# Splitting the first bank's products into upper and lower row halves in eleven pieces of a sequence transform

## The chip, the cores and the metric

The kernel runs on one core of one Trainium2 chip. The core has a matrix engine (TensorE, PE in the profile, with its weight loads listed apart as PEld), and the engines VectorE (DVE), ScalarE (ACT), GpSimd (POOL) and SyncE (SP), which issues most DMA transfers. The metric is the device time of one execution in microseconds; a smaller time is better. Times of several executions are given as a median.

## The reference

The output mixes two branches by a gate for each of 2048 tokens of 640 features. Cut to what matters:

```python
g = sigmoid((x * gate_w).sum(-1, keepdims=True))
# A: a Fourier mixing by matrices, real part of DFT_seq(DFT_hidden(x))
a = x @ dft_hid_re.T ; b = x @ dft_hid_im.T
A = dft_seq_re @ a - dft_seq_im @ b
# B: an expert layer: for 32 heads the best two of 16 + 16 keys, four candidates,
# the best two of them, softmax, and gelu(x . u[expert]) * v[expert]
out = g * A + (1 - g) * B
```

The kernel works out A in the other order, first along the sequence and then along the features. The change lies in the first of these two products, `dft_seq_re @ x`.

## The kernel before

All products are made in a split form: each operand f is held as a high part h and a rest l, both in a 32-bit matmul format, and a product is the sum of three matmuls, wh with h, wh with l and wl with h. The helper `mm3` (L141) issues the three into one PSUM bank; its lines L143, L144 and L145 are most of TensorE's work.

The sequence transform is cut into 128 pieces `n = (w, c, s)` (L170): w is the real or imaginary matrix, c one of four chunks of 512 output positions, s one of 16 blocks of 128 input tokens. In `seq_piece` a piece takes the 128 tokens as rows of the array: the weights are the tokens' features `X[s]` (128 columns for each of five feature blocks d), the moving operand is a 128 x 512 block of the matrix, h and l. Bank d (0 to 4) collects feature block d over the 16 pieces of a chunk. So a piece issues 5 x 3 = 15 matmuls, and behind the last piece of a chunk ScalarE copies each bank to a staging tile `ST`.

The first four pieces (`BYPASS`) issue their products in another order (L239), part by part over all five banks, while the inputs are still coming in. From piece 4 on the order is bank by bank.

The order of the work is written out by hand: the program's order is the order on each engine. `seq_piece(n)` issues the load for piece n + 5 (SP queue), the split for piece n + 3 (ScalarE and GpSimd), and the products of piece n; `follow(n)` then issues what a table (`at`) has put behind piece n. In the first 30 pieces that is: loading and splitting the tokens (`load_x`, `split_x`), sums for the gate (`gate_sum`, VectorE), and behind pieces 6, 9, 12, 15 and so on, up to piece 27, the weight folding `w_part`: 16 matmuls from `wq` tiles that fill 32 columns of the array each (L380, listed as 32 in the trace), whose results VectorE transposes (L386). `load_wq` (L371) fetches the next `wq` tiles into buffers that these matmuls free. From piece 31 on, steps of the expert branch are put between the pieces (`score_step`), and later products of one-hot tiles that fill 64 columns (L857).

PSUM has eight banks. Banks 0 to 4 belong to the sequence transform, 5 and 6 to `w_part`; bank 7 holds the warm-up products at the start and is taken again by the expert branch from piece 31 on. The staged results of the first chunk are multiplied by the gate on VectorE behind piece 23 (`gate_piece`, L217).

Of the kernel before, what the change touches and what calls it, by code (L numbers as in the profile page):

```python
# [17 lines left out]
P = 128  # L18
# [7 lines left out]
NT = S // P  # L26
# [15 lines left out]
AWAY = 11  # L42
BYPASS = 4
ACCUM_END = NT * (NC + 2) - 4


class Pump:
# [59 lines left out]
def gated_mix_kernel(ctx: ExitStack, tc: tile.TileContext, xT, xn, dreT, dimT, wsre, wsim, wq, kT, uT, vv, gw, out):  # L107
    nc = tc.nc
# [13 lines left out]
    def bank(n, shape=(P, TC), dt=F32):  # L122
        return psum.tile(list(shape), dt, name=f"b{n}", tag=f"b{n}")
# [9 lines left out]
    def stage():  # L133
        return ST[:, rotate("st", 5)]

    def split(f, h, l, eng):

        nc.scalar.activation(h, f, AF.Copy)  # L138
        eng.tensor_sub(l, f, h.bitcast(F32))  # L139

    def mm3(o, wh, wl, ah, al, first, last, more=False):  # L141

        nc.tensor.matmul(o, wh, ah, start=first, stop=False, skip_group_check=more)  # L143
        nc.tensor.matmul(o, wh, al, start=False, stop=False, skip_group_check=more)  # L144
        nc.tensor.matmul(o, wl, ah, start=False, stop=last, skip_group_check=more)  # L145
# [9 lines left out]
    def run_bg(us):  # L155
        bg.run(us, share)
# [14 lines left out]
    pf, psp, X, xr = {}, {}, {}, {}  # L171

    def load_piece(n):
        if n < NPC:
            w, c, s = pieces[n]
            pf[n] = big.tile([P, TC], F32, name="wf", tag="wf", bufs=5)
            nc.sync.dma_start(pf[n], (wsre, wsim)[w][c, s])  # L177
# [3 lines left out]
    def split_piece(n):  # L181
        if n < NPC:
            psp[n] = h, l = WS[:, n % 4, 0], WS[:, n % 4, 1]
            f = pf.pop(n)
            if not N0 + 4 <= n < (4 * NT if n % 2 else ACCUM_END) or 4 * NT <= n < N1 + 10:
                split(f, h, l, nc.gpsimd)
                return
            nc.scalar.activation(h, f, AF.Copy)
            nc.scalar.activation(l, h.bitcast(F32), AF.Copy, scale=-1.0)  # L189
            w, c, s = pieces[n]  # L190
            nc.gpsimd.dma_start(l, (wsre, wsim)[w][c, s], accum_op=OP.add)  # L191
# [9 lines left out]
            f()  # L201


    banks = []
    p3, last_part, ending, closing, early, share = None, False, False, False, True, 0.95
    grow, staged, P22 = {}, {}, {}

# [21 lines left out]
    def seq_piece(n):  # L229
        w, c, s = pieces[n]  # L230
        if s == 0:
            banks[:] = [bank(d) for d in range(KD)]
        load_piece(n + 5)
        split_piece(n + 3)
        h, l = psp.pop(n)
        if n < BYPASS:
            for a, (x, c) in enumerate(((0, h), (0, l), (1, h)) if n == 0 else ((0, h), (1, h), (0, l))):
                for d in range(KD):
                    nc.tensor.matmul(banks[d], X[s][:, x, d * P:(d + 1) * P], c, start=n + a == 0, stop=False)  # L239
            return  # L240
        for d in range(KD):
            ds = slice(d * P, (d + 1) * P)
            mm3(banks[d], X[s][:, 0, ds], X[s][:, 1, ds], h, l, s == 0, s == NT - 1)
            if s == NT - 1:
                staged[n // NT, d] = f = stage()
                nc.scalar.activation(f, banks[d], AF.Copy)
            run_bg(0.68)

    for q in range(2 * NC):
        n = NT * (q + 1)  # L250
# [246 lines left out]
    n = b + 2  # L497
# [20 lines left out]
    for n in range(N0):  # L518
        seq_piece(n)
        follow(n)  # L520
# [252 lines left out]
    for p in range(NP):  # L773
        n = N0 + 4 * p + min((p + 1) // 2, 3)
# [3 lines left out]
    for n in range(2 * NT + 3, 4 * NT + 3):  # L778
        s = n % NT
# [269 lines left out]
    for k, (n, m) in enumerate(((-1, 2), (0, 4), (5, 7), (7, 9), (10, 12))):  # L1049
        n, m = NT * (NC + 2) + n, NT * (NC + 2) + m  # L1050
# [181 lines left out]
    for n in range(N0, NPC):  # L1232
        ending, closing, early = n >= NPC - 7, n % NT == NT - 1, n < ACCUM_END
        seq_piece(n)
        follow(n)
        if n >= N1 and p3 is None and NT // NB - 1 in gated:
            p2_stack.close()
            p3 = ctx.enter_context(tc.tile_pool(name="p3", bufs=1, reuse_waits="tile"))
            pools.append(p3)
            HOT.append(p3.tile([P, 2, 2, 16 * E * 4], F16, name="hot0"))  # L1240
            HOT.append(p3.tile([P, 2, 2, 16 * E * 4], F16, name="hot1", tag="WP"))
            bg.add(experts(), late=True)
            bg.credit -= 3.0
        if n == NPC - 4:
            bg.drain(lambda: {2, 3} <= set(free_sets))
            HOT.pop()
            WP = p3.tile([P, 2, 2, TC], F32R, name="WP", tag="WP")
        for m in prep_split.get(n, ()):
            split_step(m)
# [54 lines left out]
```

## Time and profile before

| what | value |
|---|---|
| median of two runs | 750.96 us (750.54 and 751.38) |
| the profiled execution, first to last instruction (span) | 748.7 us |
| its own time with what lies around the span | not listed apart; the two runs are 1.8 to 2.7 us above the span |
| granted TensorE clock, mean | 0.999 |
| full-size products in L143, L144, L145 on `X` | 3 x 620 listed |
| 32-column products (L380) | 256 in 8 blocks |
| 64-column products (L857) | 512 |

The span is that of one execution which the hardware profiler recorded. In a group's row stand line, engine, operation, output from input, array rows x columns, shape and count, and then the busy time in us, the mean length of one in ns, and the idle time ahead of them. In a timeline row stand start and length in us, then engine, line, operation and count. A matmul's listed length reaches from its start to the end of its way through the array, and the next one starts well before that; the pace is the distance between starts.

### The profile page before, as it was taken

How to read it: one execution, taken by the hardware profiler on the slowest of the kernel's cores; microseconds unless marked ns; L12 is line 12 of the kernel's file. 1: busy time of each engine (PE TensorE's matmuls, PEld its weight loads, DVE VectorE, ACT ScalarE, POOL GpSimd, SP SyncE). 2: the span in 40 equal slices, each digit the busy share in tenths (PEclk: the TensorE clock that was granted, in tenths of full speed). 3: DMA queues.
4: the chain of work that ended last, by engine and by line, in shares of the span. 5: the costliest groups of instructions: out<-in, count | busy, mean ns of one | idle time of the engine just before them, and what ended most of it. 6: DMA issues, size and time to landing. Idle time of an engine off the chain costs nothing.

```text
span 748.7 us, 11141 instructions
## 1 busy us (share of the span) xinstructions
PE 743.8 (99%) x3925; PEld 603.8 (81%) x3925; DVE 585.7 (78%) x741; ACT 365.9 (49%) x664; POOL 342.4 (46%) x286
## 2 busy tenths in 40 slices
PE   9999999999999999999999999999999999999998
PEld 7777767888888888888888888888888888888887
DVE  6964098495999899999999888979899974357651
ACT  4325234543544745555463686633545653443451
POOL 5533325440532424145235456643455793487253
PEclk9999999999999999999999999999999999999999
DMA  9999999777556786972398766488876689775301
GB/s 333 392 380 364 344 374 354 231 222 250 129 176 141 190 242 157 237 200 79 114 395 285 162 168 188 133 255 280 266 234 197 222 262 343 219 239 172 113 29 71
DMA packets 84488, 171.11 MB, mean 229 GB/s; under 512 B 16080, under 2 KB 21328, under 8 KB 84176
## 3 DMA queue, kind: packets, MB, share of 16 engines
q1 hardware_dynamic: 70960, 146.13, 57.9%
q0 software_dynamic: 5472, 9.96, 8.5%
q10 hardware_dynamic: 8000, 14.31, 5.2%
q8 instruction: 31, 0.51, 0.3%
q14 instruction: 25, 0.20, 0.1%
HBM read 136.40 MB, written 32.39 MB: 225 GB/s over the span
## 4 chain that ended last, share of the span: by engine, by line
PE 94%; DMA 5%; SPq 0%; DVE 0%; ACT 0%; issue 0%; ACTq 0%
PE b L143 30%; PE b L145 30%; PE b L144 30%; PE b L239 2%; DMA wf<-in_wsre 2%; PE b L380 2%; DMA wq<-in_wq 1%; PE b L857 1%; DMA xd<-X 1%; DMA gdr<-gc 1%; DVE wp L386 0%; SPq L177 0%; ACT WS L295 0%; ACTq L514 0%; DVE ST L1191 0%
## 5 line engine op out<-in xcount | busy, mean ns | idle before, releaser
L143 PE MATMUL b<-WS,X 128*128 128x512 f32 x620 | 243.3, 392 | 0.0
L144 PE MATMUL b<-WS,X 128*128 128x512 f32 x620 | 241.4, 389 | 0.0
L145 PE MATMUL b<-WS,X 128*128 128x512 f32 x620 | 241.3, 389 | 0.0
L139 POOL TENSOR_TENSOR WS<-wf,WS 128x512 fp32r<-128x512 f32 x89 | 131.9, 1486 | 168.3 <-ACT WS L138 151.8
L143 PEld LDWEIGHTS b<-WS,X 128*128 128x128 f32 x620 | 116.3, 188 | 28.2 <-issue 4.1
L145 PEld LDWEIGHTS b<-WS,X 128*128 128x128 f32 x620 | 116.4, 188 | 24.4
L144 PEld LDWEIGHTS b<-WS,X 128*128 128x128 f32 x620 | 116.4, 188 | 23.6
L138 ACT ACTIVATE WS<-wf 128x512 fp32r<-128x512 f32 x89 | 55.5, 626 | 69.0 <-PE b L145 40.9
L845 DVE TENSOR_TENSOR hot<-rows,wtab 128x1024 f16<-128x1024 f16 x64 | 57.8, 930 | 4.3 <-PE b L857 4.3
L139 POOL TENSOR_TENSOR xl<-xf,xh 128x640 fp32r<-128x640 f32 x16 | 27.2, 1702 | 72.0 <-ACT xh L138 72.0
L567 ACT ACTIVATE sc<-b 128x512 f32<-128x512 f32 x32 | 19.9, 621 | 80.8 <-PE b L145 77.0
L191 POOL DMA_DIRECT2D WS<-in_wsre x30 | 26.4, 881 | 61.8 <-ACT WS L189 60.5
L139 POOL TENSOR_TENSOR WS<-ra,WS 128x512 fp32r<-128x512 f32 x33 | 47.1, 1439 | 14.3 <-ACT WS L138 14.1
L815 ACT ACTIVATE b<-b,mask 128x128 f32<-128x128 f32 x128 | 43.1, 342 | 14.9 <-PE b L857 11.8
L138 ACT ACTIVATE WS<-ra 128x512 fp32r<-128x512 f32 x47 | 29.4, 631 | 42.4 <-PE b L145 29.6
L622 DVE TENSOR_TENSOR eq<-sc,mm 128x1024 f16<-128x1024 f32 x32 | 44.4, 1387 | 0.9
L629 DVE TENSOR_REDUCE tied<-eq 128x64 f32<-128x1024 f16 x32 | 39.0, 1219 | 0.9
L620 DVE TENSOR_REDUCE mm<-sc 128x64 f32<-128x1024 f32 x32 | 38.7, 1211 | 0.2
L139 POOL TENSOR_TENSOR WP<-ra,WP 128x512 fp32r<-128x512 f32 x13 | 19.2, 1490 | 31.0 <-ACT WP L138 30.9
L217 DVE SCALAR_TENSOR_TENSOR ST<-ST,grow 128x512 f32<-128x512 f32 x40 | 31.7, 855 | 1.7 <-ACT tw L138 1.7
L845 DVE TENSOR_TENSOR hot<-hot,rows 128x1024 f16<-128x1024 f16 x32 | 31.6, 986 | 0.0
L143 PE MATMUL b<-WU,xh 128*128 128x512 f32 x80 | 31.1, 389 | 0.0
(209 smaller groups left out, 1449.1 us busy)
## 6 DMA issues: line engine op xcount, KB each, us to landing
X<-xd SPq DMA_DIRECT2D x36, 640.0 KB, 6.5
wq<-in_wq SPq DMA_DIRECT2D x32, 640.0 KB, 7.1
wf<-in_wsim SPq DMA_DIRECT2D x64, 256.0 KB, 4.8
wf<-in_wsre SPq DMA_DIRECT2D x63, 256.0 KB, 6.4
ra<-pd SPq DMA_DIRECT2D x40, 256.0 KB, 3.3
pd<-ST ACTq DMA_DIRECT2D x35, 256.0 KB, 5.6
WS<-in_wsre POOLq DMA_DIRECT2D x30, 256.0 KB, 6.0
xd<-X SPq DMA_DIRECT2D x11, 640.0 KB, 9.1
```

Of the source, the lines that this page charges most:

```text
L138: nc.scalar.activation(h, f, AF.Copy)
L139: eng.tensor_sub(l, f, h.bitcast(F32))
L143: nc.tensor.matmul(o, wh, ah, start=first, stop=False, skip_group_check=more)
L144: nc.tensor.matmul(o, wh, al, start=False, stop=False, skip_group_check=more)
L145: nc.tensor.matmul(o, wl, ah, start=False, stop=last, skip_group_check=more)
L191: nc.gpsimd.dma_start(l, (wsre, wsim)[w][c, s], accum_op=OP.add)
L217: nc.vector.scalar_tensor_tensor(f, f, -1.0 if w else 1.0, g, op0=OP.mult, op1=OP.mult)
L620: nc.vector.tensor_reduce(m, sc, op=OP.max, axis=AX.X)
L622: nc.vector.tensor_tensor(eq, sc, m[:, :, None].to_broadcast([P, HH, E]), op=OP.is_equal)
L629: nc.vector.tensor_reduce(tied[:, s, ib, :], eq, op=OP.add, axis=AX.X)
L815: nc.scalar.activation(f[:, :, n], f[:, :, n], AF.Copy, scale=mask4[:, n:n + 1])
L845: nc.vector.tensor_tensor(o, a, b, op=op)
```

## The change

In pieces 4 to 14 of the first chunk (`ROW_TILED`) the three products of bank 0 are cut in two by rows. The upper 64 tokens' product goes to bank 0 as before, and the lower 64 tokens' product, which works in the lower half of the array's rows, goes to bank 7, held as `lower` from piece 4 on. Upper and lower alternate in the program. Piece 15 makes full products again. At the chunk's end, behind ScalarE's copy of bank 0 to the staging tile, VectorE adds bank 7 to it. Banks 1 to 4 and all other pieces stay.

```diff
+ROW_TILED = range(BYPASS, NT - 1)
...
-    banks = []
+    banks, lower = [], []
...
+        if n == BYPASS:
+            lower.append(bank(7))
         for d in range(KD):
             ds = slice(d * P, (d + 1) * P)
-            mm3(banks[d], X[s][:, 0, ds], X[s][:, 1, ds], h, l, s == 0, s == NT - 1)
+            if d == 0 and n in ROW_TILED:
+                top, low = slice(0, P // 2), slice(P // 2, P)
+                for i in range(3):
+                    w, a = X[s][:, i // 2, ds], (h, l, h)[i]
+                    nc.tensor.matmul(banks[0], w[top], a[top], start=False, stop=False)
+                    nc.tensor.matmul(lower[0], w[low], a[low], start=i == 0 and n == BYPASS,
+                                     stop=i == 2 and n == ROW_TILED[-1])
+            else:
+                mm3(banks[d], X[s][:, 0, ds], X[s][:, 1, ds], h, l, s == 0, s == NT - 1)
             if s == NT - 1:
                 staged[n // NT, d] = f = stage()
                 nc.scalar.activation(f, banks[d], AF.Copy)
+                if d == 0 and lower:
+                    nc.vector.tensor_add(f, f, lower.pop())
```

On TensorE, at the end of piece 6, behind which a block of 32-column products stands, and the start of piece 7. Before (b_162 to b_166 are banks 0 to 4):

```order
L145 MATMUL b_166<-WS,X 128x512
L380 MATMUL b_354<-wq,kp 32x320 x4
L380 MATMUL b_359<-wq,kp 32x320 x4
L380 MATMUL b_354<-wq,kp 32x320 x4
L380 MATMUL b_359<-wq,kp 32x320 x4
L143 MATMUL b_162<-WS,X 128x512
L144 MATMUL b_162<-WS,X 128x512
L145 MATMUL b_162<-WS,X 128x512
L143 MATMUL b_163<-WS,X 128x512
```

And now, where the lines of the pair are L250 and L251 and b_279 is bank 7:

```order
L146 MATMUL b_166<-WS,X 128x512
L393 MATMUL b_364<-wq,kp 32x320 x4
L393 MATMUL b_369<-wq,kp 32x320 x4
L393 MATMUL b_364<-wq,kp 32x320 x4
L393 MATMUL b_369<-wq,kp 32x320 x4
L250 MATMUL b_162<-WS,X 128x512
L251 MATMUL b_279<-WS,X 128x512
L250 MATMUL b_162<-WS,X 128x512
L251 MATMUL b_279<-WS,X 128x512
L250 MATMUL b_162<-WS,X 128x512
L251 MATMUL b_279<-WS,X 128x512
L144 MATMUL b_163<-WS,X 128x512
```

Three products of bank 0 have become six, and here the halves follow the 32-column block directly; in eight of the eleven pieces they stand between full products on both sides.

On VectorE, at the end of the chunk (piece 15), ahead of the transposes of the next `w_part` block. Before:

```order
L509 TENSOR_SCALAR gt<-gt 128x16
L510 STREAM_TRANSPOSE gc<-gt 128x32
L386 STREAM_TRANSPOSE wp<-b_680 128x2x5x32
L386 STREAM_TRANSPOSE wp<-b_685 128x2x5x32
L139 TENSOR_TENSOR WU<-wp,WU 128x5x128
```

And now:

```order
L522 TENSOR_SCALAR gt<-gt 128x16
L523 STREAM_TRANSPOSE gc<-gt 128x32
L259 TENSOR_TENSOR ST<-ST,b_279 128x512
L399 STREAM_TRANSPOSE wp<-b_715 128x2x5x32
L399 STREAM_TRANSPOSE wp<-b_720 128x2x5x32
L140 TENSOR_TENSOR WU<-wp,WU 128x5x128
```

One addition stands ahead of the transposes, and it waits for ScalarE's copy. The order on ScalarE, GpSimd and SyncE is the one of before.

## The prediction

> **What bounds the kernel now.** I read the page's first and fourth parts, then who waited for whom on TensorE.
>
> ```profile
> PE 743.8 (99%) x3925; PEld 603.8 (81%) x3925; DVE 585.7 (78%) x741; ACT 365.9 (49%) x664; POOL 342.4 (46%) x286
> PEclk9999999999999999999999999999999999999999
> PE 94%; DMA 5%; SPq 0%; DVE 0%; ACT 0%; issue 0%; ACTq 0%
> PE b L326 <- PEq L1296: 0.8, 1, 0.8
> PE b L380 <- DMA wq<-in_wq: 0.7, 1, 0.7
> ```
>
> TensorE (PE) is busy for 743.8 of 748.7 us at an undiminished clock, it is 94% of the chain that ended last, and it waited for others for 1.5 us in all. So a microsecond added to TensorE's stream comes out at the end almost whole, and nothing that another engine saves is seen. But a busy TensorE isn't at its peak: the real pace lies in the distances between starts. The stretch below stands at the end of piece 6, which is one of the eleven that change; in it lies one block of L380, whose products fill 32 columns of the array each, four beside each other.
>
> ```profile
> 27.59 0.39 PE L145 MATMUL b<-WS,X 128*128 128x512 f32 x1
> 27.81 0.39 PE L143 MATMUL b<-WS,X 128*128 128x512 f32 x1
> 28.04 0.39 PE L144 MATMUL b<-WS,X 128*128 128x512 f32 x1
> 28.27 0.39 PE L145 MATMUL b<-WS,X 128*128 128x512 f32 x1
> 28.59 2.36 PE L380 MATMUL b<-wq,kp 128*32 128x320 f32 x32
> 30.88 0.50 PE L143 MATMUL b<-WS,X 128*128 128x512 f32 x1
> 31.21 0.40 PE L144 MATMUL b<-WS,X 128*128 128x512 f32 x1
> 31.45 0.39 PE L145 MATMUL b<-WS,X 128*128 128x512 f32 x1
> 31.68 0.40 PE L143 MATMUL b<-WS,X 128*128 128x512 f32 x1
> 31.91 0.39 PE L144 MATMUL b<-WS,X 128*128 128x512 f32 x1
> 32.14 0.39 PE L145 MATMUL b<-WS,X 128*128 128x512 f32 x1
> 32.37 0.39 PE L143 MATMUL b<-WS,X 128*128 128x512 f32 x1
> ...
> 30.51 0.43 PE L380 MATMUL b<-wq,kp 128*32 128x320 f32 x1
> ```
>
> The first column is the start. From 27.59 to 28.27 three products take 0.68 us: one full product costs 0.227 us, not the 0.39 us of its own length. The last row, the last product of the L380 block, comes from a narrower look at the same timeline.
>
> **The change, part by part.**
>
> *Removed:* in 11 pieces the three full products of the first bank, 33 x 0.227 = 7.5 us of TensorE.
>
> *Added on TensorE:* 66 products over 64 rows with the same 512 columns. A half product streams as many columns as a full one, so the change can win nothing by streaming; the question is whether the two of a pair run beside each other. No product over half of the rows stands in this trace. The nearest row is L380, with several parts of the array working at once: from 28.59 to 30.51 stand 31 steps, so 0.062 us for each product of 320 columns. At the pace of the full products (0.227 / 512 us per column) 320 columns would take 0.142 us. More than two ran at a time, then. I take it that two row halves do the same, and a pair costs about what one product costs. At most the pair is quicker by what a full product has beyond its streaming:
>
> ```profile
> L143 PE MATMUL b<-WS,X 128*128 128x512 f32 x620 | 243.3, 392 | 0.0
> L143 PE MATMUL b<-WS,ts 128*128 128x256 f32 x8 | 2.3, 283 | 0.0
> ```
>
> 256 more columns lengthen a product by 392 - 283 = 109 ns, so 512 columns are 0.218 us of the 0.227: a gain of 0.009 x 33 = 0.3 us at most. At the other end the two halves run one after the other: 33 x 0.227 = 7.5 us more. Between these I take 0.1 us for all 33 pairs, near the gainless end, since L380 is the row that is nearest in kind.
>
> *Weight loads.* Each half product loads its own 128 columns, 66 loads for 33.
>
> ```profile
> 30.87 0.19 PEld L143 LDWEIGHTS b<-WS,X 128*128 128x128 f32 x1 [0.52 <-issue]
> 30.98 0.19 PEld L144 LDWEIGHTS b<-WS,X 128*128 128x128 f32 x1
> 31.21 0.19 PEld L145 LDWEIGHTS b<-WS,X 128*128 128x128 f32 x1
> ```
>
> After the L380 block two loads start 0.11 us apart although each is listed with 0.19, so loads follow each other every 0.11 us. Two are 0.22 us and just fit under a pair of 0.227. Normally a load starts with the product before it (31.21 stands in both lists) and is hidden there. I cost it at nothing; the cover is the pair that is running. If the loads went strictly one behind the other at 0.19, a pair would take 0.38: 33 x 0.15 = 5.0 us.
>
> The Trainium skill, TensorE: Matmul & The Clock Gate, section Part 3 (packing small matmuls), gives for tiles in different row groups a span of one product and about 4 ns more; by it the 33 pairs would cost 0.13 us. The same section says that a weight load overlaps a running product only where the row groups differ. The trace disagrees for full products, whose load at 31.21 starts together with the product before it; for halves it is a rival below.
>
> *Switches of the array's layout.* This is the term that I take to decide. The L380 block shows both directions. Into it: 28.59 - 28.27 = 0.32, 0.09 more than a product's step. Out of it: a round of four takes (30.51 - 28.59) / 7 = 0.27, but from the last product to the first full one it is 30.88 - 30.51 = 0.37, 0.10 more. Then 31.21 - 30.88 = 0.33, 0.10 more than a step, since the first load wasn't made ahead (the load at 30.87 starts with its product, after 0.52 idle). The five steps from 31.21 to 32.37 take 1.16, 0.02 to 0.03 over 5 x 0.227. Out costs 0.10 + 0.10 + 0.025 = 0.22 to 0.23 us. The other product that splits the array shows the same:
>
> ```profile
> 570.72 0.39 PE L145 MATMUL b<-WS,X 128*128 128x512 f32 x1
> 571.04 0.95 PE L857 MATMUL b<-hot 128*64 128x64 f16 x48
> 571.92 0.50 PE L143 MATMUL b<-WS,X 128*128 128x512 f32 x1
> 572.25 0.39 PE L144 MATMUL b<-WS,X 128*128 128x512 f32 x1
> ...
> 571.79 0.20 PE L857 MATMUL b<-hot 128*64 128x64 f16 x1
> ```
>
> In: 571.04 - 570.72 = 0.32 again. Out: the restart 572.25 - 571.92 is 0.33 again. The step into row halves needs loads of 128 columns like the restart: 0.09 + 0.10 + 0.02 = 0.21 to 0.22. I take 0.23 for either direction.
>
> How many: each of the 11 pieces goes into the halves at its start and out after the first bank, 22 switches. Three of these pieces (7, 10, 13) stand right behind an L380 block, whose way out was paid before too; there the halves follow the 32-column tiles directly and only one switch is new. 22 - 3 = 19, and 19 x 0.23 = 4.4 us. Bounds: nothing that the trace shows is under 0.09, which gives 1.7 us; with no price at all it is nought.
>
> The Trainium skill, TensorEngine Tiling (Array Packing), section Key Properties, says that changing the tiling mode drains TensorE, and not changing the tile within a mode. The trace agrees, with 0.32 and 0.37 us where 0.227 and 0.27 are the steps. The rule gives no price, so the sum by it is the one of the rows, 4.4 us; without a drain it would be nothing.
>
> *Added on VectorE:* one addition from PSUM at the end of the chunk, and bank 7 held from piece 4 to there. Its price is in an addition of the same kind; its place is ahead of the transposes that wait for the next L380 block:
>
> ```profile
> L1114 DVE TENSOR_TENSOR ST<-ST,b 128x512 f32<-128x512 f32 x14 | 9.4, 685 | 18.5 <-ACT ST L1110 11.0 <-PE b L145 5.0 <-ACT WS L138 2.5
> 65.07 0.21 DVE L510 STREAM_TRANSPOSE gc<-gt 128x32 f32<-128x32 f32 x1
> 68.61 1.05 DVE L386 STREAM_TRANSPOSE wp<-b 128x320 f32<-128x320 f32 x2 [3.34 <-PE b L380]
> ```
>
> 0.69 us falls into an idle stretch of 3.34 us. It waits for ScalarE's copy of the first bank; behind it stand only transposes whose products come later. The result is read in piece 23 (L217), and bank 7 isn't taken again before the scores begin. Nothing. Without that cover it would be 0.69 us of VectorE, which has a fifth of its time idle.
>
> *What is given back:* TensorE waits once for a wq transfer, 0.7 us, in the last L380 block, behind the changed pieces. If the transfer keeps its time while TensorE is 4 us later, that wait goes; but the wq loads are themselves released by the products that use them:
>
> ```profile
> 104.86 1.82 PE L380 MATMUL b<-wq,kp 128*32 128x320 f32 x24
> 107.37 0.74 PE L380 MATMUL b<-wq,kp 128*32 128x320 f32 x8 [0.69 <-DMA wq<-in_wq]
> ...
> SPq L371 <- PE b L380: 22.1, 8, 5.0
> ```
>
> The queue waited 22.1 us for that, so these loads mostly move with TensorE. Between nothing and 0.7 I take 0.2 back. The other transfers and splits get more time, not less.
>
> Sum: 4.4 + 0.1 - 0.2 = 4.3 us. The profiled execution's span goes from 748.7 to 753.0 us. The two timed runs took 750.54 and 751.38 us, so 1.8 to 2.7 us lie around the span, and the change doesn't touch them. Against the median of 750.96 the forecast is **755.3 us**. Two per cent, about what a measurement of this kernel tells from no change, is 15.0 us: the forecast is slower but within it.
>
> **The rivals.**
>
> *A, cheap switches.* If row halves only drain, with their loads made ahead, or if the layout doesn't count as another, a switch is 0.09 at most: 19 x 0.09 = 1.7 us, some of it given back, 752.5 us. Against it: both blocks of split products pay the restart. Chance 0.12.
>
> *B, loads not hidden.* In the halves a load waits until its own rows are free, while the other half runs beside it: 0.11 x 33 = 3.6 us more, 758.9 us. For it: 2 x 0.11 leaves hardly any room under 0.227. Against it: full products load under a running product in the same rows. The rule of the Trainium skill cited above on row groups would bring this about. Chance 0.10.
>
> *C, the change doesn't do what it says.* The halves run in turn: 7.5 us more, 762.8 us. Against it: L380's 0.062 us for 320 columns; for it: those are column tiles, each with all 128 rows, and no row tile was ever seen here. Chance 0.12.
>
> *D, the other side: slower by over 2%.* Every half product behaves like the first one after a switch, 0.33 from start to start with its load in the open, and the halves run in turn: 66 x 0.33 = 21.8 us for 7.5, 14.3 more, and 4.3 on top, less 11 x 0.10 that the entries already hold: 17.5 us, 768.5 us. It decides from 0.29 us per half product on (7.5 + 15.0 - 4.3 + 1.1 = 19.3 over 66). Against it: inside the L380 block the loads lie under running products. Chance 0.05.
>
> **How the numbers follow.** The forecast keeps 0.61. A, B and C lie within 2%. The range goes from 751.5 (A with the whole 0.7 given back and the 0.3 of quicker pairs: 1.7 - 1.0 = 0.7) to 763.2 (C with its 0.2 not given back, and the 0.2 by which the sum may be rounded); D and the edges of A and C stay outside. The likeliest case's own range is 753.5 to 756.5. Faster by over 2%: no case gives it, 0.01 for the unforeseen. Slower by over 2%: D, 0.05. Within: 0.94.
>
> **What would show it.** In the profile after, the two lines of a pair (its upper and its lower half) start within 0.02 us of each other and the next pair 0.23 later; pair starts 0.45 apart would be C, 0.33 with the loads idle before them B or D. The first pair of a piece should start 0.32 after the last full product, and the first full product behind the pairs should be followed by a step of 0.33. Eleven first banks should take 0.68 + 0.4 us each. The addition should stand in an idle stretch of VectorE. TensorE's wait for wq should be 0.7 or less. I would be wrong by most if a half product can't start while the other half runs, or if a switch into row halves costs another multiple of the full drain.

## The result and the profile after

| | before | after |
|---|---|---|
| median of the runs, us | 750.96 (2 runs) | 754.92 (754.72 and 755.12) |
| span of the profiled execution, us | 748.7 | 752.9 |
| ratio of times | 1 | 1.0057, 95% interval 1.0041 to 1.0073 |

The change makes the kernel slower by 0.6%, 4.0 us by the medians and 4.3 us by the two spans before rounding (748.66 and 752.94). The lines of the page of after that answer to those of before (shares of the span; engines of the chain), and who waited for whom on TensorE:

```profile
PE 748.9 (99%) x3958; PEld 603.8 (80%) x3958; DVE 585.5 (78%) x742; ACT 366.3 (49%) x664; POOL 344.7 (46%) x286
PEclk9999999999999999999999999999999999999999
PE 99%; DVE 0%; issue 0%
PE b L339 <- PEq L1309: 0.8, 1, 0.8
```

TensorE bounds the kernel as before, with 33 products more and 5.1 us more busy time, and no wait for wq is listed any more. The timeline of TensorE at the first changed piece (4), and its weight loads over the same stretch (start and length in us; L250 is an upper half, L251 a lower one, L144 to L146 are full products):

```profile
19.33 0.49 PE L250 MATMUL b<-WS,X 64*128 64x512 f32 x1
19.33 0.49 PE L251 MATMUL b<-WS,X 64*128 64x512 f32 x1
19.67 0.39 PE L250 MATMUL b<-WS,X 64*128 64x512 f32 x1
19.67 0.40 PE L251 MATMUL b<-WS,X 64*128 64x512 f32 x1
19.90 0.39 PE L250 MATMUL b<-WS,X 64*128 64x512 f32 x1
19.90 0.39 PE L251 MATMUL b<-WS,X 64*128 64x512 f32 x1
20.22 0.50 PE L144 MATMUL b<-WS,X 128*128 128x512 f32 x1
20.56 0.40 PE L145 MATMUL b<-WS,X 128*128 128x512 f32 x1
20.80 0.39 PE L146 MATMUL b<-WS,X 128*128 128x512 f32 x1
...
19.33 0.18 PEld L250 LDWEIGHTS b<-WS,X 64*128 64x128 f32 x1 [0.35 <-issue]
19.33 0.18 PEld L251 LDWEIGHTS b<-WS,X 64*128 64x128 f32 x1
19.44 0.19 PEld L250 LDWEIGHTS b<-WS,X 64*128 64x128 f32 x1
```

The two halves of a pair start in the same hundredth of a microsecond, their loads too; from the second pair to the third it is 0.23 us, one step of a full product. What costs time stands at the ends. The load at 19.33 comes after 0.35 us in which none was issued, and 19.67 - 19.33 = 0.34 is 0.11 over a step. Behind the last pair the first full product starts 20.22 - 19.90 = 0.32 later, 0.09 over a step, and the next one 0.34 after that. These are about the prices that the 32-column blocks showed in the trace of before (0.09 on the way in, 0.10 and 0.10 on the way out).

What this comes to is read between two marks that both kernels have: the start of piece 4 and the start of the fourth 32-column block, which stands behind all changed pieces. Before, then after:

```profile
18.29 0.39 PE L143 MATMUL b<-WS,X 128*128 128x512 f32 x1
66.72 2.36 PE L380 MATMUL b<-wq,kp 128*32 128x320 f32 x32
118.48 2.36 PE L380 MATMUL b<-wq,kp 128*32 128x320 f32 x32
...
71.82 2.36 PE L393 MATMUL b<-wq,kp 128*32 128x320 f32 x32
109.96 2.46 PE L393 MATMUL b<-wq,kp 128*32 128x320 f32 x32
122.78 2.36 PE L393 MATMUL b<-wq,kp 128*32 128x320 f32 x32
```

Before it is 66.72 - 18.29 = 48.43 us, after 71.82 - 19.33 = 52.49, and 0.09 more for the first switch, which lies ahead of 19.33: the change costs 4.15 us of TensorE there, 0.218 for each of 19 switches. The rest of the 4.3 us between the two spans is made of two terms of opposite sign. Piece 4 began 19.33 - 0.09 - 18.29 = 0.95 us later in the profile of after, ahead of any changed instruction. And from the fourth block to the eighth it was 51.76 us before and 50.96 after, 0.8 less: the wait for wq in the seventh block, of which this execution kept only 0.1 (the row at 109.96, 2.46 us long where the others have 2.36). 0.95 + 4.15 - 0.8 = 4.3.

### The profile page after: what moved, and what is told of

It is laid out like the page before. It is cut to its first block, busy times and chain, and to the rows that moved or that the text cites. A ratio compares the mean times of both kernels' runs of the same rounds, so it can differ in the third digit from the quotient of the medians.

```text
span 752.9 us, 11208 instructions
## 1 busy us (share of the span) xinstructions
PE 748.9 (99%) x3958; PEld 603.8 (80%) x3958; DVE 585.5 (78%) x742; ACT 366.3 (49%) x664; POOL 344.7 (46%) x286
## 4 chain that ended last, share of the span: by engine, by line
PE 99%; DVE 0%; issue 0%
PE b L144 31%; PE b L145 30%; PE b L146 30%; PE b L393 2%; PE b L240 2%; PE b L250 1%; PE b L870 1%; PE b L339 1%; DVE ST L1204 0%; PE b L251 0%
## 5 line engine op out<-in xcount | busy, mean ns | idle before, releaser
L144 PE MATMUL b<-WS,X 128*128 128x512 f32 x609 | 240.4, 395 | 0.0
L145 PE MATMUL b<-WS,X 128*128 128x512 f32 x609 | 237.5, 390 | 0.0
L146 PE MATMUL b<-WS,X 128*128 128x512 f32 x609 | 237.4, 390 | 0.0
L144 PEld LDWEIGHTS b<-WS,X 128*128 128x128 f32 x609 | 114.4, 188 | 29.9 <-issue 6.6
L146 PEld LDWEIGHTS b<-WS,X 128*128 128x128 f32 x609 | 114.4, 188 | 23.9
L145 PEld LDWEIGHTS b<-WS,X 128*128 128x128 f32 x609 | 114.5, 188 | 22.8
L858 DVE TENSOR_TENSOR hot<-rows,wtab 128x1024 f16<-128x1024 f16 x64 | 61.5, 986 | 2.6 <-PE b L870 2.6
```

Of the source, the lines that this page charges most:

```text
L858: nc.vector.tensor_tensor(o, a, b, op=op)
```

## The experiments

All ratios are against the kernel before, run on the same chip as the experiment. My theory was that the time goes into the switches of the array's layout, with the pairs themselves costing one product each. The rivals were a price of the pairs, of their loads, or of the addition, and products that run beside each other for another reason than their rows.

**Fewer switches, same pairs.** The first bank goes last in the even pieces, so that the pairs of two neighbouring pieces adjoin.

```diff
-        for d in range(KD):
+        for d in (1, 2, 3, 4, 0) if n in ROW_TILED and n % 2 == 0 else range(KD):
```

> In the even pieces 4 to 14 the first bank goes last, so that the halves of two neighbouring pieces stand behind each other: the same 33 pairs, but 12 additional switches of the array's layout where the change has 19. Theory (the change costs its switches, about 0.21 us each, and the pairs nothing): 12 x 0.21 = 2.5 us over before, so about 1.5 us under the change, ratio 1.0025 to 1.0040. Rival (each pair costs about 0.12 us): 4 us as in the change, ratio 1.0055. In the profile: isolated groups of pairs are gone but for piece 14, and a pair that follows another starts 0.23 us behind it.

Measured: 752.58 us against 750.45, ratio 1.0030 (1.0019 to 1.0040). The marks on TensorE, the first with a full product since piece 4 now begins with bank 1, and between them a place where two pieces' pairs adjoin:

```profile
19.22 0.39 PE L144 MATMUL b<-WS,X 128*128 128x512 f32 x1
70.31 2.36 PE L393 MATMUL b<-wq,kp 128*32 128x320 f32 x32
...
22.60 0.39 PE L250 MATMUL b<-WS,X 64*128 64x512 f32 x1
22.60 0.39 PE L251 MATMUL b<-WS,X 64*128 64x512 f32 x1
22.83 0.39 PE L250 MATMUL b<-WS,X 64*128 64x512 f32 x1
```

51.09 us between the marks, 2.66 over before, is 0.222 for each of 12 switches. The first pair of piece 5 (22.83) starts 0.23 behind the last of piece 4 (22.60). With the pairs' number unchanged the price fell by 1.49 us, so it does not hang on the pairs.

**Five times the pairs, two switches.** All banks of the eleven pieces are made of halves; the lower ones all go to bank 7, so that their share is missing from the sums of banks 1 to 4.

```diff
-            if d == 0 and n in ROW_TILED:
+            if n in ROW_TILED:
...
-                    nc.tensor.matmul(banks[0], w[top], a[top], start=False, stop=False)
-                    nc.tensor.matmul(lower[0], w[low], a[low], start=i == 0 and n == BYPASS,
-                                     stop=i == 2 and n == ROW_TILED[-1])
+                    nc.tensor.matmul(banks[d], w[top], a[top], start=False, stop=False)
+                    nc.tensor.matmul(lower[0], w[low], a[low], start=i == d == 0 and n == BYPASS,
+                                     stop=i == 2 and d == 4 and n == ROW_TILED[-1])
```

> All five banks of pieces 4 to 14 are made of pairs; all lower halves go to bank 7, so the sums come out in the wrong bank for four of five. 165 pairs in place of 33, but only 2 additional switches (into the halves at piece 4, out at piece 15; the 32-column blocks are switches as before). Theory: 2 x 0.21 = 0.4 us over before, at most 1 us, ratio 1.0000 to 1.0015. Rival (pairs cost 0.12 us each): 20 us over before, ratio 1.026. Rival (weight loads barely fit under a pair): pairs more than 0.235 apart and 1.3 us or more for the 165.

Measured: 750.66 us against 750.45, ratio 1.0005 (0.9996 to 1.0013). The groups of halves by line, and the marks:

```profile
L250 PE MATMUL b<-WS,X 64*128 64x512 f32 x165 | 38.6, 389 | 0.0
L251 PE MATMUL b<-WS,X 64*128 64x512 f32 x165 | 38.6, 389 | 0.0
...
18.72 0.49 PE L250 MATMUL b<-WS,X 64*128 64x512 f32 x1
67.56 2.36 PE L393 MATMUL b<-wq,kp 128*32 128x320 f32 x32
```

48.84 us between the marks and 0.09 ahead of them: 0.5 us over before for two switches, while 165 full products have become 330 halves. At 0.22 for each switch 0.06 us is left for all 165 pairs: a pair costs one product, and its two loads are hidden. Both rivals that charge the pairs fall.

**The halves in turn.** The three uppers stand ahead of the three lowers, in two loops in place of one.

```diff
                     nc.tensor.matmul(banks[0], w[top], a[top], start=False, stop=False)
+                for i in range(3):
+                    w, a = X[s][:, i // 2, ds], (h, l, h)[i]
                     nc.tensor.matmul(lower[0], w[low], a[low], start=i == 0 and n == BYPASS,
```

> As the change, but in each piece the three upper halves go first and the three lower ones behind them. Theory (neighbours in the program run beside each other when they lie in different rows, and the order of starts is the program's): only the last upper and the first lower half overlap, 5 steps of 0.227 for 3, so 2 x 0.227 x 11 = 5.0 us over the change, 9 us over before, ratio 1.011 to 1.013. Rival (the array reorders freely between the halves): as the change, 1.0055. Rival (a change of the half is itself a stop): 6 steps and a drain, over 12 us, ratio 1.016 or more.

Measured: 754.21 us against 750.45, ratio 1.0046 (1.0032 to 1.0059). My expectation missed, and the rival that the array reorders between the halves held: no slower than the change. TensorE at piece 4 (L250 upper, L253 lower):

```profile
18.89 0.49 PE L250 MATMUL b<-WS,X 64*128 64x512 f32 x1
18.90 0.49 PE L253 MATMUL b<-WS,X 64*128 64x512 f32 x1
19.23 0.39 PE L250 MATMUL b<-WS,X 64*128 64x512 f32 x1
19.24 0.39 PE L253 MATMUL b<-WS,X 64*128 64x512 f32 x1
...
71.46 2.36 PE L395 MATMUL b<-wq,kp 128*32 128x320 f32 x32
```

The first lower half is the fourth product in the program, and it starts ahead of the second. Between the marks it is 71.46 - 18.89 = 52.57 us, less than 0.1 over the change's 52.49. So products in free rows pass products that wait for busy ones. How far that reaches was the question of a later run.

**Without the addition.** The two lines with `tensor_add` are left out, and with them the lower halves' share of the first bank.

> As the change without the addition at the chunk's end, so the lower halves are missing from the result. Theory (the addition lies in VectorE's idle time): as the change within 0.3 us, ratio 1.0055. Rival (it delays the transposes and through them TensorE): 0.7 us less, ratio 1.0045. In the profile VectorE's idle time ahead of the transposes of that block is 0.7 us longer.

Measured: 754.60 us against 750.45, ratio 1.0052 (1.0036 to 1.0068). In the groups below stands VectorE of after, then of this kernel, between the gate's last operation and the transposes:

```profile
68.78 0.21 DVE L523 STREAM_TRANSPOSE gc<-gt 128x32 f32<-128x32 f32 x1
69.84 0.69 DVE L259 TENSOR_TENSOR ST<-ST,b 128x512 f32<-128x512 f32 x1 [0.85 <-ACT ST L257]
73.72 1.05 DVE L399 STREAM_TRANSPOSE wp<-b 128x320 f32<-128x320 f32 x2 [3.18 <-PE b L393]
...
68.23 0.21 DVE L521 STREAM_TRANSPOSE gc<-gt 128x32 f32<-128x32 f32 x1
72.70 1.05 DVE L397 STREAM_TRANSPOSE wp<-b 128x320 f32<-128x320 f32 x2 [4.26 <-PE b L391]
...
18.32 0.49 PE L250 MATMUL b<-WS,X 64*128 64x512 f32 x1
70.81 2.36 PE L391 MATMUL b<-wq,kp 128*32 128x320 f32 x32
```

With the addition VectorE still idles 3.18 us behind it and then waits for TensorE's product, so nobody waits for the addition. The marks are 52.49 us apart, the same as in after. The idle stretch did not grow by 0.7 as I had expected but from 4.03 to 4.26, because the gate's operations came at another time relative to TensorE; the verdict rests on the marks.

**Both halves in the same rows.** The second product of each pair takes the upper 64 rows as well, so that the lower 64 tokens' share is left out of the sum.

```diff
-                top, low = slice(0, P // 2), slice(P // 2, P)
+                top, low = slice(0, P // 2), slice(0, P // 2)
```

> As the change, but the second product of each pair uses the upper 64 rows too, for weights and moving operand, so that the lower 64 tokens are left out of the sum and the upper ones counted twice over the two banks. Theory (a pair costs one product only because its halves lie in different rows): six steps of 0.227 us per piece for three, 3 x 0.227 x 11 = 7.5 us over the change, 11.6 us over before, ratio 1.0155; loads stay hidden. Rival (two banks are enough for products to run beside each other): as the change, 1.0055. Rival (loads of the same rows aren't hidden): 0.1 us more for each of 66, ratio over 1.024.

Measured: 762.34 us against 750.27, ratio 1.0154 (1.0137 to 1.0172). TensorE at piece 4, and the second mark:

```profile
19.19 0.49 PE L250 MATMUL b<-WS,X 64*128 64x512 f32 x1
19.52 0.39 PE L251 MATMUL b<-WS,X 64*128 64x512 f32 x1
19.76 0.39 PE L250 MATMUL b<-WS,X 64*128 64x512 f32 x1
19.99 0.39 PE L251 MATMUL b<-WS,X 64*128 64x512 f32 x1
...
79.24 2.36 PE L393 MATMUL b<-wq,kp 128*32 128x320 f32 x32
```

The products follow each other in the program's order, 0.33 us apart behind the switch and 0.23 to 0.24 from then on; 60.05 us between the marks, 7.56 more than in after. That is the 33 x 0.227 = 7.5 us that rival C charged. It is the different rows that let a pair run as one: different banks alone are not enough. Whether two halves in different rows could share one bank was not run. The loads are hidden even though they go to rows in which a product is running.

**Far halves.** All banks in halves as in the second experiment, but 15 uppers first and then 15 lowers in each piece.

```diff
+        if n in ROW_TILED:
+            for half, r in enumerate((slice(0, P // 2), slice(P // 2, P))):
+                for d in range(KD):
...
+                        nc.tensor.matmul(lower[0] if half else banks[d], w[r], a[r],
...
+            return
```

> As the kernel with all five banks in halves (all lower ones into bank 7, so the sums of four banks are wrong), but in each piece the 15 upper halves stand first and the 15 lower ones behind them. In the run where three uppers stood ahead of three lowers the array paired them all the same. If it looks 15 products ahead (30 with their weight loads): as with neighbours, 0.5 us over before, ratio 1.000 to 1.002. If it looks only a few ahead: up to 15 steps of 0.227 more per piece, 37 us over before, ratio 1.05; between these the starts in the profile show how far it looks.

Measured: 775.09 us against 750.27, ratio 1.0325 (1.0303 to 1.0347), between the two limits that I had set. The first 30 halves from piece 4 on, which the timeline lists in one row, and the second mark:

```profile
18.68 6.03 PE L250 MATMUL b<-WS,X 64*128 64x512 f32 x30
91.40 2.36 PE L403 MATMUL b<-wq,kp 128*32 128x320 f32 x32
```

The mark stands at 91.40 with piece 4 starting at 18.68, 24.4 us over before with the 0.09 ahead of piece 4. Less 0.5 for the switches it is 23.9 us, or 9 to 10 exposed steps in each of 11 pieces on average, where 15 would be no overlap at all. In the single starts of the trace the first one that follows another by a few ns is the 13th of piece 4 (21.333 behind 21.325). Upper and lower halves share a line here, so which is which is read from the order: 11 uppers run alone, the twelfth runs beside the first lower one, and three uppers are still waiting. The same comes again at the next border, where the first upper half of piece 5 starts at 23.982 beside the twelfth lower one of piece 4 (23.975); so fewer than 11 steps are exposed in a piece. The array looked past about three waiting products, not past more. (A few records may be missing in a trace, so three is not exact.)

**Both kernels once more.**

> The kernel before, unchanged, for a second profile. Theory (the first 20 us and the one wait for wq differ from execution to execution, by the step of the clock's release and by the transfers): the start of piece 4 moves by up to 1 us and the waits for wq by up to 1.5 us against the first profile, while the stretch from piece 4 to the fourth block of 32-column products stays the same to 0.01 us. Rival (the later start belongs to the change): the start of piece 4 at 18.3 us again.

> The change, unchanged, against before in more rounds. Theory: 19 switches of 0.218 us are 4.15 us; the wait for wq gives back between nothing and 0.8: ratio 1.0045 to 1.0055.

The kernel before took 751.69 us in one execution, with a span of 749.9. The change took 754.83 us against 750.27, ratio 1.0052 (1.0038 to 1.0065). Marks of before again (start of piece 4, fourth block) and its wait, and then the marks of the change again:

```profile
18.92 0.39 PE L143 MATMUL b<-WS,X 128*128 128x512 f32 x1
67.90 2.36 PE L380 MATMUL b<-wq,kp 128*32 128x320 f32 x32
PE b L380 <- DMA wq<-in_wq: 0.8, 2, 0.4
...
18.96 0.49 PE L250 MATMUL b<-WS,X 64*128 64x512 f32 x1
71.45 2.36 PE L393 MATMUL b<-wq,kp 128*32 128x320 f32 x32
```

The unchanged kernel started piece 4 at 18.92 in place of 18.29, so the late start does not belong to the change, and the rival falls. In one point the expectation missed: between the marks it took 48.98 us, 0.55 over its first profile, since one of its two waits for wq now fell inside the third block (a step of 0.77 us there in place of 0.25), while the first profile had its only one in the seventh. The change again has 52.49 us between its marks, to the hundredth.

## Why the prediction was right

The forecast was 755.3 us and the time 754.92, inside the likeliest case's own range; the forecast case held, and its steps can be checked one by one.

- *Pairs cost what a product costs:* right, and shown from both sides. With 165 pairs and two switches the kernel is 0.5 us over before on TensorE; with both halves in the same rows it is the 7.5 us of rival C. I had taken this from column tiles, the nearest row; row tiles behave alike.
- *Weight loads are hidden:* right, for another reason than mine. I let two loads follow each other 0.11 us apart under one pair; in the trace of after the two loads of a pair start together. Rival B, for which the Trainium skill's rule in TensorE: Matmul & The Clock Gate, Part 3, on loads and row groups would speak, falls: the pairs of after follow each other every 0.23 us, and so do the products of the kernel with both halves in the same rows.
- *Switches decide, 19 of them at 0.23:* right in number and nearly in size. They cost 4.15 us, 0.218 each; the kernel with 12 switches has 0.222 each, the one with 2 has 0.25. This term too was transferred, from 32- and 64-column tiles to row halves, and the count is borne out by the three kernels: about one price fits 19, 12 and 2. Rival A falls, since row halves pay the restart too.
- *The addition is covered:* right, by the marks that don't move without it.
- *0.2 us given back by the wait for wq:* mis-sized for the profiled execution, which got 0.8 back. The wait of before also stands in the seventh of the eight blocks (the row at 107.37), not in the last as I wrote; both lie behind the changed pieces. But this wait differs from one execution to the next: 0.7 us in one place in the first profile of before, twice 0.4 in the second, 0.5 in the second profile of the change, none listed in the first. It isn't shown that the change gives any of it back; the ratios of 1.0057, 1.0052 and 1.0046 (in turn) lie around the 1.0055 that 4.15 us alone would make, and can't tell 0.2 us.
- *Not in my sum:* the later start of 0.95 us in the profile of after. It and the lost wait cancelled, so the span came out at 752.9 where I had 753.0; that nearness is partly luck. What sets the start is told in the last section. Two smaller slips decide nothing: by its own terms the range should have begun at 750.96 + 0.7 = 751.7 rather than 751.5, and the time around the span, which I put at 1.8 to 2.7 us, is 1.7 to 1.8 us where a run's own span is listed (755.12 and 753.4, 754.72 and 752.9); the 2.7 set one execution's time against another's span.

No version faster than before came out of this: halves of a full 128-row product stream as many columns as the product, so the best that the second experiment shows is no change (0.9996 to 1.0013).

## What to carry to other kernels

Cutting a full product into row halves costs nothing by itself and wins nothing; what counts is how often the array changes its layout, here about 0.22 us each way, so products of one layout belong beside each other. To price a change on a saturated TensorE, measure between two marks on that engine that both traces have: the spans of two executions differed by 0.95 us at the start and 0.8 in a transfer, each about a fifth of the effect.

## What was unexpected

Products don't always start in the program's order: a lower half that stood fourth started 0.01 us behind the first (18.89 and 18.90), ahead of two uppers that waited for their rows. With 15 uppers in front it didn't reach that far, and the price was 24 us.

The first products of an execution don't always run at full pace. In the stretch from 4.60 to 6.90 us before had ten products under way and after only eight (the columns are busy time and count of TensorE and of its loads, then the other engines, the granted clock, the DMA share and GB/s):

```profile
4.60:6.90 2.30, 2.30 (x10) 1.88 (x11) 1.42 (x3) 0.86 (x2) 0.00 (x0) 1.00 0.96 333
4.60:6.90 2.30, 2.30 (x8) 1.87 (x7) 1.93 (x4) 1.59 (x3) 0.00 (x0) 1.00 0.97 337
```

In the second row the steps between the first starts are 0.43 us in place of 0.23. The views give the granted clock as 1.00 in both, but they count the time ahead of the first clock record as full. The kept traces hold where that record starts: the clock is granted in full from 3.68 us on in the profile of before and from 6.52 on in that of after. The steps fall at that moment (in after the start at 6.48 is the last that follows another by 0.43), in all ten profiles, with the moment between 3.43 and 6.52.

Piece 4 starts later where the moment comes later: at 18.3 us where it is 3.43 or 3.68, at 18.7 where it is 5.1 to 5.2, at 18.9 to 19.0 where it is 5.6 to 5.8, at 19.2 to 19.3 where it is 6.2 to 6.5. A kernel with halves stands at either end (18.32 in the one without the addition, 19.33 in after), so the late start goes with the clock and not with the change. The Trainium skill, TensorE: Matmul & The Clock Gate, Part 1, tells of a clock at half rate until a window of activity that runs freely, not from the kernel's start, has passed. The traces agree: 0.43 is about twice 0.23, the moment differs between two profiles of one kernel (3.68 and 5.82 in before), and the stretch of full clock lasts 744.106, 747.519, 750.932, 754.345 or 767.999 us in the ten profiles, lengths that differ by whole steps of 3.413 us.
